# Attention and top-1 expert FFN on one core: the early experts' PSUM tiles, the first FFN rows' transposes, and the start of the weight stream

## The chip, the cores and the metric

The kernel runs on one core of a Trainium2 chip, in one launch. The metric is the device time of that core in microseconds (us), as the median of several runs. Each engine (TensorE = PE, VectorE = DVE, ScalarE = ACT, GpSimd = POOL, SyncE = SP) works through its own instructions in the order in which they were written, and waits at an instruction until the semaphores that it names have come.

## The reference

Long-range attention (a window of 32 keys to each side, plus 8 global positions) on 8 batches x 8 heads x 576 positions x 64, and then a feed-forward layer (FFN) in which each of the 4608 tokens goes to the one expert of eight with the highest logit:

```
x = attention(q, k, v)                      # 4608 rows of 512
logits = x @ w_gate;  e = argmax(logits);  g = softmax(logits)[e]
h = relu(x[rows of e] @ w1[e])              # 512 -> 1024
out[rows of e] = g * (h @ w2[e])            # 1024 -> 512
```

## The kernel before

**Attention and routing.** 36 steps of 128 query rows (lines 829 to 956) compute scores, exponentials and the weighted sum. Each step's output `xn` is transposed on PE (`xt_of`, line 487) and multiplied with the gate's weights (`gate`, `gates`), and a group of up to four steps is routed: DVE finds the maximum, `ranks` counts rows by expert with matmuls, `route2` turns counts into slots, `place` and `chunk` build one-hot matrices, `slots` adds them (on PE into a `tr_s` tile, then on DVE) into `acc`, a table from expert and slot to the row's place. `store` writes the rows to a scratch in DRAM, `xrow_scr`; `gather` (line 719) fetches the rows of a 128-row chunk with an indirect DMA from POOL, and `yscatter` (line 750) writes results to their tokens in the same way.

**Early experts.** The first 256 rows of experts 0 and 1 are known before the attention ends. Their FFN, `wave()` (line 779), is written as a generator, and `waves(n)` advances it by n pieces between the last groups' routing (lines 959 to 1002). A piece is one `hp` block (four matmuls of 256 columns and a relu on ACT, 16 in all) or half a `yw` block (four of eight matmuls of 512 columns, four blocks in all, each scaled by ACT into `y1`). The `hp` blocks rotate over three PSUM banks, of which two are halves of one tile; the four `yw` blocks take turns in the two banks of one tile:

```python
scw = scp.tile([128, 2, 512], FP32, tag="sc", name="hp")
hps = [scw[:, 0], gqp.tile([128, 512], FP32, tag="g", name="hp"), scw[:, 1]]
xw = xp.tile([128, 2, 512], FP32, tag="x", name="yw")
```

`wrows(i)` (line 969) transposes their gathered rows on PE into `tr_w` and copies them on ACT to `xts1`.

**From the wave to the FFN.** When the last groups are in `acc`, DVE computes `idx` (line 1001), the rows of every remaining chunk. After the wave, five weight pieces are fetched (`fetch`, line 1046: two DMAs of 256 KB from SP into an `st` tile), two chunks each of experts 0 and 1 are gathered, the wave's results are scattered, and expert 0's two chunks are transposed (`xtrans`, line 733, into `tx`) and copied by DVE to `xts`, which the first `h` matmul reads.

**The main FFN** (line 1209) goes over the eight experts: eight `h` blocks (fb 0 to 7, relu on ACT for even and on DVE for odd ones), between them the transposes for the next expert, then a `yp` block for each chunk (two chunks for experts 0 and 1, four for the others). From expert 2 on, `castp` (line 1053) casts a loaded piece to fp16 after odd fb and after each `yp` block, on ACT or DVE in turn, and fetches the next: 40 pieces for experts 3 to 7. `overflow_plan()` (line 1107), a generator too, works out on DVE which 128-row blocks are left beyond 512 rows of an expert; the loop advances it by one step after each fb in expert 2 and by two in experts 3 and 4. Its late steps transpose `acc` (line 1191), build three small `sel` matrices and multiply them on PE into `yi` (line 1199). The blocks left over run after the loop, in a chain of conditional parts (line 1305).

## Time and profile before

| | us |
|---|---|
| runs: lowest, median, highest of three | 393.03, 395.82, 397.62 |
| the profiled execution | 391.89 |
| its span, first to last instruction | 390.2 |
| PE busy, share of the span | 349.4 (90%) |
| DVE busy | 236.9 (61%) |
| POOL busy | 225.0 (58%) |
| ACT busy | 183.9 (47%) |

In the profile's rows a time is counted from the span's start. The row of a group of matmuls ends with the drain of its last one, in which the next row already begins. The idle time of an engine stands in brackets with what ended it; a wait for several semaphores is put down to the one that came last by the profile, which need not be the one that it stood for.

### The profile page before, as it was taken

Reading aid. Unit: us, or ns where it says so; the run is one execution under the profiler, and the core shown is the slowest. Engines: PE = TensorE matmul, PEld = TensorE weight load, DVE = VectorE, ACT = ScalarE, POOL = GpSimd, SP = SyncE. Lnnn points to the kernel's source line nnn. Section 1 sums busy time; section 2 is a strip of 40 time slices with the busy share of each in tenths; the row PEclk is TensorE's granted clock in tenths of the full one; section 3 lists DMA queues with packets and bytes.
Section 4 is the critical chain, followed back from the end, with each engine's and each line's share of the span. In section 5 each row is a group of like instructions: output and inputs, shape, how many; then the busy total and the mean of one; then the engine's idle time right before and its main releaser. Section 6 shows DMA issues by size and latency. Waiting matters only on the chain.

```text
span 390.2 us, 13139 instructions
## 1 busy us (share of the span) xinstructions
PE 349.4 (90%) x5290; PEld 224.7 (58%) x5290; DVE 236.9 (61%) x632; ACT 183.9 (47%) x310; POOL 225.0 (58%) x315
## 2 busy tenths in 40 slices
PE   6988989799898998989978878999899999999990
PEld 2557667566676776766656635654354444455550
DVE  8876876464957558777557504675875654333340
ACT  6636365553645455564535622264454445233330
POOL 8632676590746445394949466766466663565451
PEclk9999999999989999999999999999999999999997
DMA  7996969972899427999998885369999999132011
GB/s 192 225 256 114 270 114 235 229 181 62 181 271 212 130 67 164 260 204 203 169 166 169 166 252 188 109 203 360 356 342 355 368 372 329 37 117 83 22 38 49
DMA packets 90276, 76.29 MB, mean 196 GB/s; under 512 B 44380, under 2 KB 84956, under 8 KB 90208
## 3 DMA queue, kind: packets, MB, share of 16 engines
q1 hardware_dynamic: 79168, 54.34, 54.8%
q0 software_dynamic: 11040, 21.02, 21.6%
q8 instruction: 44, 0.72, 0.8%
q14 instruction: 24, 0.20, 0.2%
HBM read 68.62 MB, written 15.64 MB: 216 GB/s over the span
## 4 chain that ended last, share of the span: by engine, by line
PE 65%; DVE 10%; DMA 7%; issue 7%; POOL 6%; SPq 1%; ACT 1%; POOLq 0%; DVEq 0%
PE x L459 13%; PE yp L1242 12%; PE h L1224 11%; PE gx L546 5%; PE sc L459 4%; PE tr_x L491 4%; DMA wall<-in_k_dram 2%; PE poh L1275 2%; PE tr_k L524 2%; PE tr_l L506 2%; DMA wall<-in_q_dram 2%; PE tr_qk L340 2%; PE tr_qk L342 2%; POOL out_dram L751 2%; DVE xn L483 1%
## 5 line engine op out<-in xcount | busy, mean ns | idle before, releaser
L329 POOL CAST wall<-wall 128x768 f16<-128x768 f32 (+1 forms) x52 | 46.1, 903 | 40.5 <-DMA wall<-in_k_dram 23.6
L462 ACT ACTIVATE wall<-sc 128x1024 f32<-128x1024 f32 x36 | 36.9, 1025 | 54.4 <-PE sc L459 49.4
L682 POOL TENSOR_SCALAR hota<-ioc,chk,rowv 128x32 f16<-128x32 f16 (+8 forms) x33 | 34.4, 1070 | 36.1 <-DVE sm L654 36.0
L1224 PE MATMUL h<-xts,wall 128*128 128x512 f16 (+1 forms) x256 | 53.8, 352 | 0.8 <-DVE xts L741 0.8
L1242 PE MATMUL yp<-wall,ht 128*128 128x512 f16 x224 | 49.8, 379 | 1.7 <-DVE ht L764 1.7
L459 PEld LDWEIGHTS x<-wall 128*64 128x64 f32 x1152 | 37.6, 139 | 17.4 <-issue 15.5
L459 PE MATMUL x<-wall 128*64 128x65 f32 x1152 | 42.9, 227 | 3.1 <-issue 2.4
L751 POOL DMA_INDIRECT out_dram<-y,xr x24 | 25.1, 1048 | 24.5 <-DVE y L748 17.3
L1242 PEld LDWEIGHTS <-ht 128*128 128x128 f16 x224 | 21.5, 98 | 26.9 <-DVE ht L764 2.5
L1224 PEld LDWEIGHTS <-wall 128*128 128x128 f16 x256 | 23.9, 98 | 20.2 <-DVE xts L741 1.0
L481 DVE RECIPROCAL rz<-x 128x8 f32<-128x8 f32 x36 | 7.4, 207 | 42.3 <-PE x L459 42.1
L764 DVE TENSOR_SCALAR ht<-h 128x512 f16<-128x512 f32 (+1 forms) x32 | 19.9, 623 | 20.0 <-PE h L1224 18.1
L721 POOL DMA_INDIRECT xr<-xrow_scr,idx x24 | 25.9, 1080 | 9.0 <-POOL xr L720 9.0
L483 DVE TENSOR_TENSOR xn<-x,rz 128x512 f32<-128x512 f32 x36 | 24.9, 692 | 3.1
L766 ACT ACTIVATE ht<-h 128x512 f16<-128x512 f32 (+1 forms) x32 | 17.4, 542 | 19.1 <-PE h L1224 17.0
L492 ACT ACTIVATE xt<-tr_x 128x512 f32<-128x512 f32 (+1 forms) x37 | 22.0, 594 | 8.6 <-PE tr_x L491 8.5
L491 PE MATMUL tr_x<-id,xn 128*128 128x128 f32 x144 | 22.7, 280 | 3.7 <-DVE xn L483 3.6
L715 ACT ACTIVATE wall<-st 128x1024 f16<-128x1024 f32 x20 | 21.0, 1051 | 10.4 <-DMA st<-in_moe_w_dram 10.4
L459 PE MATMUL x<-vgd,ek 64*64 64x260 f32 x288 | 24.7, 404 | 0.0
L344 DVE COPY qt<-tr_qk 128x576 f16<-128x576 f16 x32 | 23.8, 750 | 0.7
L574 ACT ACTIVATE x16b<-xn 128x512 f16<-128x512 f32 x36 | 22.9, 636 | 0.0
L347 ACT ACTIVATE kt<-tr_qk 128x576 f16<-128x576 f16 x32 | 20.5, 646 | 4.6 <-PE tr_qk L342 4.6
(296 smaller groups left out, 702.1 us busy)
## 6 DMA issues: line engine op xcount, KB each, us to landing
st<-in_moe_w_dram SPq DMA_DIRECT2D x80, 256.0 KB
wall<-in_k_dram SPq DMA_DIRECT2D x32, 288.0 KB
wall<-in_q_dram SPq DMA_DIRECT2D x32, 288.0 KB
wall<-in_v_dram SPq DMA_DIRECT2D x24, 256.0 KB
wall<-in_moe_w_dram POOLq DMA_DIRECT2D x24, 256.0 KB, 6.9
xrow_scr<-x16b SPq DMA_DIRECT2D x8, 516.0 KB
wall<-in_v_dram SPq DMA_DIRECT2D x16, 192.0 KB
xg<-xgs SPq DMA_DIRECT2D x64, 2.0 KB
```

The lines of the kernel that those rows point to most:

```text
L329: eng.tensor_copy(o, i_)
L344: nc.vector.tensor_copy(qt[b % 2][:, pair, :].rearrange("p (a r) -> p a r", r=R), ps[:, 0:768].rearrange("p (r a) -> p a r", r=R)[:, 32:12 ...
L459: nc.tensor.matmul(out=o, lhsT=lhsT, rhs=rhs, start=first[r, g] == i, stop=final[r, g] == i)
L462: nc.scalar.activation(out=eb[s % 2].rearrange("p r t c q -> p r (t c q)"), in_=sc, func=AF.Exp, scale=0.125)
L483: nc.vector.tensor_tensor(out=xn.rearrange("p (c r d) -> p r c d", c=4, r=2), in0=x4[:, :, :, 0:D], in1=rz.rearrange("p r (c o) -> p r c o ...
L491: nc.tensor.transpose(out=ps[:, 128 * c : 128 * c + n], in_=xn[:, 128 * c : 128 * c + 128], identity=id32[0:n, 0:n])
L574: nc.scalar.activation(out=self.x16[:, s - self.s0, 0:DM], in_=xn, func=AF.Copy)
L682: eng.tensor_scalar(out=h[:, 0 : E * n].rearrange("p (e n) -> p e n", e=E), in0=ioc[:, :, 0:n], scalar1=self.chk[:, j : j + 1], scalar2=ro ...
L721: d_ = nc.gpsimd.indirect_dma_start(out=xr.bitcast(I16), out_offset=None, in_=xrow, in_offset=IndirectOffsetOnAxis(ap=ix, axis=0), bounds_ ...
L751: d_ = nc.gpsimd.indirect_dma_start(out=out, out_offset=IndirectOffsetOnAxis(ap=xr[:, DM : DM + 2].bitcast(I32), axis=0), in_=y, in_offset ...
L1224: nc.tensor.matmul(out=ps, lhsT=w1v[:, e, c, 128 * fb : 128 * fb + 128], rhs=xts[:, c, 0:N], start=(c == 0), stop=(c == 3))
L1242: nc.tensor.matmul(out=ps, lhsT=ht[:, fc, 128 * j : 128 * j + 128], rhs=w2v[:, e, fc, :], start=(fc == 0), stop=(fc == 7))
```

## The change

It makes six edits.

1. Four one-bank PSUM tiles (pool `ps_w`) take the place of the three tiles of the wave: every `hp` and `yw` block takes the next of the four. The pools are opened in another order for this.
2. The transpose of the last step's `xn` (`xt_of`) stands ahead of the first two `wrows`; one wave piece follows instead of two, then `gate` and the routing of the last group ahead of `wrows(2)` and `wrows(3)`. The pieces are counted out 1, 3, 6, 1 instead of 2, 3, 5, 2.
3. The gathers for experts 0 and 1 are written before the rest of the wave, and expert 0's two chunks are transposed at the end of the wave, the first ahead of the last `yw` block and the second behind it, through `tr_w` tiles into a fixed place in the weights' buffer (`xts0`).
4. The first five weight pieces are fetched one by one in experts 0 and 1 (after fb 3 and 7, and after expert 0's first `yp` block). Each waits for a one-column memset of its `st` tile on DVE.
5. The plan's steps: one after each of fb 0 to 6 in expert 2; from expert 3 on two after even fb, one after odd, none after fb 7.
6. In the FFN the pool of `tx` tiles is opened first.

```diff
-        scw = scp.tile([128, 2, 512], FP32, tag="sc", name="hp")
-        hps = [scw[:, 0], gqp.tile([128, 512], FP32, tag="g", name="hp"), scw[:, 1]]
         for e in range(NW):
             for fb in range(8):
-                ps = hps[(8 * e + fb) % 3][:, 0:HALF]
+                ps = wvp.tile([128, 512], FP32, tag="w", name="hp")[:, 0:HALF]
...
-        xw = xp.tile([128, 2, 512], FP32, tag="x", name="yw")
         for e in range(NW):
             for j in range(2):
-                ps = xw[:, j, :]
+                ps = wvp.tile([128, 512], FP32, tag="w", name="yw")
...
+    apx.close()
+    wvp = aps.enter_context(tc.tile_pool(name="ps_w", bufs=4, space=PS))
...
+    xt_of(xn, xt4[:, (NS - 1) % GB])
     wrows(0)
     wrows(1)
-    xt_of(xn, xt4[:, (NS - 1) % GB])
-    waves(2)
-    wrows(2)
-    wrows(3)
+    waves(1)
     gate(xt4[:, (NS - 1) % GB], tail.lg[:, 1, :])
     tail.route1()
     tail.block(NS - 1, xn)
+    wrows(2)
+    wrows(3)
     waves(3)
...
-    waves(5)
+    waves(6)
     done.slots()
-    waves(2)
+    waves(1)
     tail.slots()
...
-    waves(99)
+    for i in range(2 * NW):
+        gather(xr01[2 * NW + i], idx[:, i // 2, 2 + i % 2 : 3 + i % 2])
+    waves(11)
+    for j in range(2):
+        ps = trp.tile([128, 4, 128], FP16, tag="tr", name="tr_w")
+        xtrans(xr01[2 * NW + j], xts0[:, :, 128 * j : 128 * j + 128], ps)
+        waves(2)
+    for i in range(2 * NW):
+        yscatter(y1[i], xr01[i])
...
+            if len(loaded) < NST and len(pieces) >= 8 * (E - 3) - NST:
+                nc.vector.memset(st[:, 0:1], 0.0)
             wload(*p_, st)
...
-    for _ in range(NST):
-        fetch()
-    rows_of = {0: gathers(0), 1: gathers(1)}
-    for i in range(2 * NW):
-        yscatter(y1[i], xr01[i])
-    xts = fp2.tile([128, 4, 512], FP16, tag="xts", name="xts")
-    for j in range(NJ[0]):
-        xtrans(rows_of[0][j], xts[:, :, 128 * j : 128 * j + 128])
+    rows_of = {0: xr01[4:6], 1: xr01[6:8]}
+    xts = xts0
...
-            for _ in range(min(e - 1, 2) if e >= 2 else 0):
+            for _ in range(0 if e < 2 or fb == 7 else 1 if e == 2 or fb % 2 else 2):
                 next(plan, None)
             if fb % 2:
+                if e < 2 and fb % 4 == 3:
+                    fetch()
...
             yout(ps, rows_of[e][j], "act" if j % 2 else "dve")
+            if e == 0 and j == 0:
+                fetch()
```

At the start of the wave, ACT (`tr_w` are the gathered rows of the early experts, `tr_x` the last step's `xn`, `hp` the wave's relus, `x16b` a copy for the store) before:

```order
L739 ACTIVATE wall<-tr_w 128x4x128 x2
L492 ACTIVATE xt_84<-tr_x 128x512
L766 ACTIVATE wall<-hp 128x256 x2
L739 ACTIVATE wall<-tr_w 128x4x128 x2
L574 ACTIVATE x16b_81<-xn 128x512
L766 ACTIVATE wall<-hp 128x256 x3
L616 ACTIVATE ex<-d 128x16
L617 ACTIVATE x16b_81<-tokt 128x2
L766 ACTIVATE wall<-hp 128x256 x11
```

and after the change:

```order
L494 ACTIVATE xt_84<-tr_x 128x512
L741 ACTIVATE wall<-tr_w 128x4x128 x2
L768 ACTIVATE wall<-hp 128x256
L576 ACTIVATE x16b_81<-xn 128x512
L741 ACTIVATE wall<-tr_w 128x4x128 x2
L768 ACTIVATE wall<-hp 128x256 x3
L618 ACTIVATE ex<-d 128x16
L619 ACTIVATE x16b_81<-tokt 128x2
L768 ACTIVATE wall<-hp 128x256 x12
```

The copy of `tr_x` moves ahead of the first two `tr_w` copies, and only one relu instead of two stands ahead of the next two.

At the end of the wave, DVE (`idx` are the rows to gather, `xr` the row buffers of the main FFN, `ht` the relus of expert 0, `xts` the transposed rows of expert 1, `st` a weight piece) before, where the first two `xts` copies are those of expert 0:

```order
L731 SCALAR_TENSOR_TENSOR idx<-acc,idf 128x32
L1004 TENSOR_TENSOR cnt<-base_115,ebasef 128x8
L741 COPY xts<-tx 128x4x128 x2
L1037 MEMSET xr 128x258 x4
L764 TENSOR_SCALAR ht<-h 128x256
L741 COPY xts<-tx 128x4x128
L764 TENSOR_SCALAR ht<-h 128x256
L741 COPY xts<-tx 128x4x128
L764 TENSOR_SCALAR ht<-h 128x256 x2
L748 TENSOR_SCALAR y<-yp,wall 128x512
```

and after:

```order
L733 SCALAR_TENSOR_TENSOR idx<-acc,idf 128x32
L743 COPY wall<-tr_w 128x4x128 x2
L1013 TENSOR_TENSOR cnt<-base_115,ebasef 128x8
L1043 MEMSET xr 128x258 x4
L766 TENSOR_SCALAR ht<-h 128x256
L743 COPY xts<-tx 128x4x128
L766 TENSOR_SCALAR ht<-h 128x256
L1057 MEMSET st 128x1
L743 COPY xts<-tx 128x4x128
L766 TENSOR_SCALAR ht<-h 128x256 x2
L1057 MEMSET st 128x1
L750 TENSOR_SCALAR y<-yp,wall 128x512
```

Expert 0's two copies now come from `tr_w`; the row of 2 holds both, though PE has a `yw` block between their transposes. The small memsets that release the weight pieces stand behind relus of expert 0.

In the main FFN, DVE at the end of the plan (`acct` is the transposed `acc`, `ht` a relu, `wall<-st` a weight cast, `ov<-yi` reads the product), in expert 4 before:

```order
L1192 COPY acct<-tx 96x384
L1195 TENSOR_SCALAR sel<-ovs,colp 96x39
L764 TENSOR_SCALAR ht<-h 128x512
L1195 TENSOR_SCALAR sel<-ovs,colp 96x39 x2
L741 COPY xts<-tx 128x4x128
L1200 CAST ov_5330<-yi 128x39
L730 TENSOR_SCALAR lt<-ov_5330 128x39
L731 SCALAR_TENSOR_TENSOR ovi<-ov_5330,lt 128x39
L1203 CAST ovei<-ove 128x39
```

and in expert 5 after:

```order
L1194 COPY acct<-tx 96x384
L1197 TENSOR_SCALAR sel<-ovs,colp 96x39
L766 TENSOR_SCALAR ht<-h 128x512
L1197 TENSOR_SCALAR sel<-ovs,colp 96x39
L719 CAST wall<-st 128x1024
L743 COPY xts<-tx 128x4x128
L1197 TENSOR_SCALAR sel<-ovs,colp 96x39
L1202 CAST ov_5335<-yi 128x39
L732 TENSOR_SCALAR lt<-ov_5335 128x39
L733 SCALAR_TENSOR_TENSOR ovi<-ov_5335,lt 128x39
```

The third `sel` step now has a relu, a weight cast and an `xts` copy between it and the first, and nothing stands between it and the read of `yi`, whose matmuls follow directly behind an `h` block on PE.

## Rows read from the trace of the kernel before

**Rows 1.** The chain that ended last, in order of time (start us, us, what).
```profile
231.63 5.61 DMA out_dram<-wall
237.27 0.77 DVE xts L741 x2
```

**Rows 2.** Timeline of PE (start us, us, engine line op tiles xcount [idle before <-releaser]).
```profile
214.13 1.03 PE L786 MATMUL hp<-wall 128*128 128x256 f16 x8 [0.24 <-ACT wall L739]
...
229.59 1.89 PE L795 MATMUL yw<-wall 128*128 128x512 f16 x8 [0.82 <-ACT wall L746]
...
236.69 0.61 PE L737 MATMUL tx<-idh,wall 128*128 128x128 f16 x8
238.08 1.05 PE L1224 MATMUL h<-xts,wall 128*128 128x256 f16 x8 [0.78 <-DVE xts L741]
238.96 0.39 PE L737 MATMUL tx<-idh,wall 128*128 128x128 f16 x4
...
253.52 1.89 PE L1224 MATMUL h<-xts,wall 128*128 128x512 f16 x8
```

**Rows 3.** Waits of PE, 205 to 245 us (who <- whom: us in total, times, longest).
```profile
PE yw L795 <- ACT wall L746: 2.4, 3, 0.8
PE hp L786 <- ACT wall L766: 2.1, 5, 0.5
```

**Rows 4.** Timeline of DVE and of ACT around the early FFN.
```profile
211.68 0.69 DVE L483 TENSOR_TENSOR xn<-x,rz 128x512 f32<-128x512 f32 x1
...
225.02 0.19 DVE L731 SCALAR_TENSOR_TENSOR idx<-acc,idf 128x32 int32<-128x32 int16 x1
...
213.98 0.59 ACT L492 ACTIVATE xt<-tr_x 128x512 f32<-128x512 f32 x1
214.76 0.82 ACT L766 ACTIVATE wall<-hp 128x256 f16<-128x256 f32 x2 [0.20 <-PE hp L786]
...
236.94 0.69 ACT L746 ACTIVATE wall<-yw,wall 128x512 f32<-128x512 f32 x1 [2.03 <-PE yw L795]
```

**Rows 5.** Timeline of POOL: a gather, the last early scatter, a gather for expert 2.
```profile
225.98 1.14 POOL L721 DMA_INDIRECT wall<-xrow_scr,idx  x1 [6.96 <-DVE cnt L1004]
...
237.90 0.98 POOL L751 DMA_INDIRECT out_dram<-wall  x1 [1.73 <-ACT wall L746]
...
239.65 1.08 POOL L721 DMA_INDIRECT xr<-xrow_scr,idx  x1 [0.27 <-POOL xr L720]
```

**Rows 6.** Row gathers issued at 224 to 239 us, then 238 to 262.
```profile
DMA to landing us min/median/max: 5.3/6.2/6.3
...
DMA to landing us min/median/max: 2.7/2.9/3.6
```

**Rows 7.** Stretch 238 to 242 us: each engine's busy us, clock, DMA share, GB/s.
```profile
238.00:242.00 4.00, 3.89 (x38) 3.38 (x39) 3.05 (x10) 1.17 (x4) 3.45 (x9) 1.00 0.31 101
```

**Rows 8.** Expert 3: timeline of DVE, then of PE.
```profile
278.68 0.68 DVE L764 TENSOR_SCALAR ht<-h 128x512 f16<-128x512 f32 x1
...
279.42 5.57 PE L1242 MATMUL yp<-wall,ht 128*128 128x512 f16 x25 [1.72 <-DVE ht L764]
```

**Rows 9.** DVE: a step of the plan in expert 4, then expert 5.
```profile
290.69 0.23 DVE L1195 TENSOR_SCALAR sel<-ovs,colp 96x39 f16<-96x39 f32 x1
...
303.77 0.69 DVE L764 TENSOR_SCALAR ht<-h 128x512 f16<-128x512 f32 x1 [0.86 <-PE h L1224]
304.37 0.69 DVE L717 CAST wall<-st 128x1024 f16<-128x1024 f32 x1
```

**Rows 10.** Weight casts of experts 5 and 6 on ACT and DVE, then PE.
```profile
308.97 1.06 ACT L715 ACTIVATE wall<-st 128x1024 f16<-128x1024 f32 x1 [1.57 <-DMA st<-in_moe_w_dram]
...
325.76 1.06 ACT L715 ACTIVATE wall<-st 128x1024 f16<-128x1024 f32 x1 [2.31 <-DMA st<-in_moe_w_dram]
...
323.81 0.69 DVE L717 CAST wall<-st 128x1024 f16<-128x1024 f32 x1 [0.75 <-DMA st<-in_moe_w_dram]
...
329.30 1.89 PE L1224 MATMUL h<-xts,wall 128*128 128x512 f16 x8
```

More of the change, by code (lines that the diff above doesn't have):

```diff
@@ L110 @@
     aps = ExitStack()
-    scp = aps.enter_context(tc.tile_pool(name="ps_sc", bufs=1, space=PS))
-    xp = aps.enter_context(tc.tile_pool(name="ps_x", bufs=1, space=PS))
+    trp = aps.enter_context(tc.tile_pool(name="ps_tr", bufs=3, space=PS))
     gqp = aps.enter_context(tc.tile_pool(name="ps_g", bufs=1, space=PS))
-    trp = aps.enter_context(tc.tile_pool(name="ps_tr", bufs=3, space=PS))
+    apx = ExitStack()
+    scp = apx.enter_context(tc.tile_pool(name="ps_sc", bufs=1, space=PS))
+    xp = apx.enter_context(tc.tile_pool(name="ps_x", bufs=1, space=PS))
     qt = [ap_.tile([128, 4, S], FP16, name=f"qt{i}") for i in range(2)]
@@ L134 @@
     y1 = [wflat[:, kf_at + 1024 * i : kf_at + 1024 * (i + 1)].bitcast(FP32) for i in range(2 * NW)]
+    xts0 = wflat[:, 3 * 8192 : 3 * 8192 + 1024].rearrange("p (c n) -> p c n", c=4)
     xr01 = [wflat[:, 8 * 8192 - ROW * (i + 1) : 8 * 8192 - ROW * i] for i in range(8)]
@@ L981 @@
     tail.block(NS - 1, xn)
+    wrows(2)
+    wrows(3)
     waves(3)
     early.slots()
+    tail.ranks()
     tail.exps()
-    tail.ranks()
     tail.route2()
@@ L1015 @@
     fst = ctx.enter_context(tc.tile_pool(name="fst", bufs=NST))
+    pst = ctx.enter_context(tc.tile_pool(name="ps_t", bufs=2, space=PS))
     psh = ctx.enter_context(tc.tile_pool(name="ps_h", bufs=3, space=PS))
     psy = ctx.enter_context(tc.tile_pool(name="ps_y", bufs=3, space=PS))
-    pst = ctx.enter_context(tc.tile_pool(name="ps_t", bufs=2, space=PS))
     def new_rows():
@@ L1029, in gathers @@
         for j in range(NJ[e]):
-            if e < NW:
-                xr = xr01[2 * NW + 2 * e + j]
-            else:
-                xr = new_rows()
-                if fresh[0]:
-                    fresh[0] -= 1
-                    nc.vector.memset(xr, 0.0)
+            xr = new_rows()
+            if fresh[0]:
+                fresh[0] -= 1
+                nc.vector.memset(xr, 0.0)
             gather(xr, idx[:, e, NJ[5] - NJ[e] + j : NJ[5] - NJ[e] + j + 1])
```

## The prediction

> **What bounds the kernel now.** I read the page first: PE is busy for 90% of the span, so a gain has to come from the few places where it stands still or works late. The chain that ended last runs through PE nearly everywhere; in the passage from the early experts to the main FFN it leaves PE for a DMA of 5.61 us that "ends" at DVE's `xts` copy [rows 1]. That is one of several semaphores on which the copy waits. PE's timeline gives the nearer reason: the `tx` transposes begin at 236.69, at once behind the last `yw` block, and the copy starts 0.58 us later, about what a copy takes to follow its transposes [rows 1, 2]. So the passage is bound by PE's own order, and the question is why the wave ends so late.
>
> The waits answer that: three `yw` blocks wait 2.4 us in total for ACT's scaling of the block before, and five `hp` blocks 2.1 us for a relu [rows 3]. Each stands for a tile, not for data: the `yw` block at 229.59 writes the other bank of the tile that ACT is still reading [rows 2]. A wait costs more than its row, because the idle time is counted from the drain of the last matmul. The drain is 0.17: the `h` row at 238.08 lasts 1.05, yet the next row begins 0.88 later [rows 2]. A block of four 256-column matmuls is thus worth 0.44 and one of eight 512-column ones 1.72 (1.89 less 0.17, as at 229.59).
>
> **Part by part. One-bank tiles.** Three `yw` waits, 2.4 + 3 x 0.17 = 2.9; five `hp` waits, 2.1 + 5 x 0.17 = 2.95; together 5.9. What comes next in their place is ACT: two relus take 0.82, so 0.41 each against 0.44 for a block, and a scaling 0.69 against 1.72 [rows 4]. With four banks a block needs the evacuation of four blocks ago, so I leave nothing of the 5.9, except 0.2 in which the last group's ranks wait for DVE's one-hot rows, which now lie closer. Bounds: all 5.9 goes, or the `hp` half stays (2.95).
>
> **The last step's transpose sooner.** It needs `xn`, which DVE ends at 211.68 + 0.69 = 212.37; PE would start it at 212.5 and ACT copy it from 213.2 on, against 213.98 before [rows 4]. But the first two `tr_w` copies now stand behind it on ACT: three copies of about 0.55 (0.59 less overlap) end at 214.85, so the first `hp` starts at 214.9 instead of 214.13 [rows 2]: +0.8, with only one block instead of two ahead of the last group's `gate`. Bounds -0.2 to +1.0.
>
> **Transposes inside the wave.** Before, 1.39 us lie between the last `yw` block and the first `h` (236.69 to 238.08). Now one group of four transposes (0.22) stands ahead of the last `yw` block. Behind it come 0.22 for the other and then the later of two things: DVE's copy, and ACT's scaling of the last `yw` block, whose bank the first `h` takes over. The scaling ended 0.94 behind the block (236.94 + 0.69 - 236.69) [rows 2, 4], so `h` follows at about 1.0; 0.22 + 1.0 against 1.39 is -0.2.
>
> The two transposes must find their rows. `idx` is ready at 225.21 and the first gather starts 0.77 later [rows 4, 5]. The last group's table comes after ten `hp` blocks that no longer wait, by my count 1.6 earlier, so the first gather starts at 224.4 and the second, 1.5 later, at 225.9. Without weights in flight a gather landed 2.7 to 3.6 us after its issue, with them 5.3 to 6.3 [rows 6]. The second is wanted at about 231.8: three us of room at 2.9, and 0.4 too late at the worst 6.3. I take 0.
>
> Wave and passage together: -5.9 + 0.2 + 0.8 - 0.2 = -5.1, and the first `h` moves from 238.08 to 233.0.
>
> **Weight pieces later.** Five memsets of one column cost DVE nothing beside its idle time there. The fifth piece is released in the second expert, at about 233.0 + 7.7 + 3.7 = 244.4 (an early expert takes (253.52 - 238.08) / 2 = 7.7 [rows 2]). Expert 2 begins at 248.4 and casts that piece after eight `h` blocks of 0.86 and its first `yp` block, over 8 us later. The DMA share of 0.31 between 238 and 242 [rows 7] says that there is room for five pieces, so I take 0. What hides it is the slack of the stream: its pieces land 2.1 us apart ((325.76 - 308.97) / 8), and the last `w1` piece of expert 7 is cast at 324.5, 4.8 us before PE wants it at 329.30 [rows 10].
>
> POOL gains less than PE: its four scatters follow the four gathers, so the last moves from 237.90 to about 234.0, and the first gather for expert 2 from 239.65 to 235.8 [rows 5]. Expert 1 wants that row at 233.0 + 7.7 + 0.9 = 241.6, and the fourth, issued 1.4 apart and used 1.1 apart, with 4.9 us of room. At a landing of 2.9 nothing is late; at 6.3 the last is late by 1.4. What the trace shows with weights in flight is five pieces at once, which is not the case here, so I take 0 and keep 1.4 as the bound. The Trainium skill (DMA: Bandwidth & Descriptors, section "Issuing engines are not separate DMA queues") says that transfers of SP and of POOL run on the same DMA engines and interleave. By that rule the pieces that no longer slow the first gathers may slow these; the two rows on landings agree with it, and the sum would be 1.4 smaller.
>
> **The plan's steps.** In expert 3 PE waits 1.72 (1.9 with the drain) at the `yp` block because DVE reaches the last relu only at 278.68 [rows 8]. Of the fourteen steps ahead of that relu the last four (1.4 us) now come later, but the heavy six before them remain, and DVE meets the relu of fb 3 with less behind it and waits for the block. I count 0.5 gained; bounds 0 to 1.4.
>
> In expert 5 there is a new wait. Two steps at fb 4 bring the third `sel` and, directly after it, the `yi` matmuls on PE. On DVE that `sel` stands behind relu, second `sel`, cast and `xts` copy of fb 3. From the relu's start (303.77): 0.60 to the next, 0.15, 0.60 for the cast, 0.34 for the copy and 0.23 for the step [rows 9] give 305.69. PE leaves fb 3 at 303.6 and reaches `yi` after 0.22 + 0.86, at 304.7. The `h` blocks queued behind it wait too: +1.05. Bounds: 0 if PE is late by as much already, 1.5 if the cast waits for its piece. The `yi` and `acc` matmuls themselves only move from expert 4 to 5.
>
> **Sum.** -5.1 - 0.5 + 1.05 = -4.55. The profiled execution took 391.89 (span 390.2 and 1.7 around it), which makes 387.3. The median of the three runs lies 3.93 above that execution; from it the forecast is 395.82 - 4.55 = 391.3.
>
> **Rivals.** (a) *Expert 2's gathers come late.* For it: POOL moves by 3.9 and PE by 5.1. Against: 4.9 us of room and a landing of 2.9. Price 1.4: 392.7.
>
> (b) *The plan is spread as smoothly as it looks.* No stall at `yi`, and the whole 1.9 of expert 3 goes: -5.1 - 1.9 = -7.0, 388.8. For it: DVE waits for PE at the relu before (0.86 idle [rows 9]). Against: the order on DVE, where relu and cast stand ahead of the third `sel`.
>
> (c) *The passage hangs on the rows, as the chain says.* Then only the 1.6 of `idx` counts: -1.6 - 0.5 + 1.05, 394.8. For it: the 5.61 of rows 1. Against: PE began `tx` without waiting for any row [rows 2].
>
> (d) *Slower: the weight stream starts too late.* If the five pieces don't land before expert 2, the stream, which sets its own pace of 2.1, is behind by up to 5 x 2.1 = 10.5 in experts 5 and 6, and casts that wait on ACT and DVE hold up the relus behind them; three `h` banks cover two blocks, 1.7. That adds up to 8.8 and gives 395.82 - 4.55 + 8.8 = 400.1. It decides from about three missing pieces on, where 6.3 exceeds the slack of 4.8. For it: casts of experts 5 and 6 waited 0.75 to 2.31 already [rows 10]. Against: the count above, 4 us between the last release and expert 2. The Trainium skill (Trainium Kernel Development and Optimization, section "Best Practices") asks to overlap DMA with compute, which a later start gives up; by it this rival would be likelier, but the share of 0.31 says that the DMAs have idle time where the pieces go now.
>
> **Chances and range.** Forecast 0.55, own range 390 to 392.5; (a) 0.14; (b) 0.14; (c) 0.10; (d) 0.07. A measurement tells about 1%, here 3.96 us, from no change; three quarters of the forecast's cases pass it (it gains 4.55), and (b) does: 0.41 + 0.14 = 0.55 faster. The rest, (a) and (c) make 0.38 within 1%; (d) is the 0.07 slower. The range of 387.5 to 395.5 holds (a), (b), (c) and the spread of the runs, and leaves out (d).
>
> **What would show it.** Right: no PE wait on ACT in `yw` and `hp`; first `h` near 233; expert 3's stall near 1.2; a new PE wait of about 1 at `yi` in expert 5. Wrong: PE waits at `tx` in expert 1 (a), at `tr_w` ahead of the last `yw` (c), or in experts 5 to 7 behind casts that wait for pieces (d).

## The result and the profile after

Seven runs of the changed kernel gave a median of 389.88 us (388.25 to 396.82), seven of the kernel before 396.04 (391.56 to 398.42): ratio 0.9869, interval 0.983 to 0.9909, so 6.2 us by the medians and 5.2 by the ratio. The ratios, here and below, leave out every run that took over 1.5% more than the fastest of its kernel. The forecast was 391.3, in a range of 387.5 to 395.5. The profiled execution after, however, took 390.4 (span 388.7), only 1.5 less than the profiled one before. Both differences have to be explained.

First the waits of PE in the changed kernel, which answer to [rows 3] (who waits for whom: us in total, times, longest), from 205 to 245 us and then from 245 to 345.

```profile
PE hp L786 <- DMA wall<-in_moe_w_dram: 1.2, 1, 1.2
PE h L1226 <- ACT wall L748: 0.6, 1, 0.6
...
PE yp L1246 <- DVE ht L766: 1.0, 1, 1.0
PE yi L1201 <- DVE sel L1197: 1.0, 1, 1.0
PE tx L739 <- DVE st L1057: 0.5, 1, 0.5
```

The eight waits on ACT between blocks of the wave are gone. The first `h` waits 0.60 for ACT's scaling, as forecast; expert 3's stall is 1.00 instead of 1.72 [rows 8]; the new wait at `yi` is 0.97. Not forecast is the wait of 0.5 at `tx` in expert 1. Its row names a one-column memset on DVE, which happened to end at about the same time. What these transposes read are the rows of the fourth gather for expert 2, issued at 243.09 and landed 5.0 later, at 248.09; e5 below shows that it is the gather. But the first `h` comes at 235.75, not at 233.0. PE's timeline answers to [rows 2] (start us, us, engine line op tiles xcount [idle before <-releaser]):

```profile
211.31 1.04 PE L501 MATMUL tr_l<-wg,xt 128*128 128x8 f32 x8
212.72 0.63 PE L493 MATMUL tr_x<-id,xn 128*128 128x128 f32 x4 [0.37 <-DVE lg L502]
213.18 0.61 PE L739 MATMUL tr_w<-idh,wall 128*128 128x128 f16 x8
215.01 0.92 PE L786 MATMUL hp<-wall 128*128 128x256 f16 x4 [1.22 <-DMA wall<-in_moe_w_dram]
215.72 1.72 PE L501 MATMUL tr_l<-wg,xt 128*128 128x8 f32 x8
...
235.75 1.03 PE L1226 MATMUL h<-wall 128*128 128x256 f16 x8 [0.60 <-ACT wall L748]
...
248.15 0.40 PE L739 MATMUL tx<-idh,xr 128*128 128x128 f16 x4 [0.49 <-DVE st L1057]
```

The `hp` block at 215.01 starts where the forecast put it (214.9). Its wait of 1.22 is put down to a weight DMA, but it stands for ACT's copies of `tr_w`, the last of which ended at 213.88 + 1.08 = 214.96:

```profile
213.88 1.08 ACT L741 ACTIVATE wall<-tr_w 128x512 f16<-128x512 f16 x2
```

Then PE is slow: a group of `tr_l` matmuls of one form took 1.04 at 211.31 and takes 1.72 at 215.72. The windows say why (length; busy us and instruction counts of PE, PEld, DVE, ACT and POOL; then the granted clock, the DMA share and GB/s):

```profile
211.00:215.00 4.00, 2.42 (x34) 2.16 (x30) 3.52 (x17) 1.66 (x4) 4.00 (x6) 1.00 1.10 170
215.00:222.00 7.00, 6.99 (x42) 5.76 (x42) 2.15 (x10) 3.33 (x9) 4.23 (x4) 0.51 0.96 183
222.00:230.00 8.00, 8.00 (x64) 6.06 (x62) 3.88 (x19) 4.99 (x13) 2.21 (x3) 1.00 0.16 50
```

Behind two pauses, 0.37 and 1.22, TensorE was granted 0.51 for seven microseconds: nearly all of it at its lower level, 1.2 GHz instead of 2.4. That costs 7 x 0.49 = 3.4 of work at full clock, and the profiled execution before had nothing like it there. Below, "lost clock" is this sum: the length of a stretch times one minus its granted clock.

Landings of the row gathers answer to [rows 6] (issues, count, median us to landing): the early rows' and some of expert 2's, 224 to 239 us, then expert 2's, 238 to 244.

```profile
wall<-xrow_scr,idx POOLq DMA_INDIRECT x4, 2.6
out_dram<-wall POOLq DMA_INDIRECT x4
xr<-xrow_scr,idx POOLq DMA_INDIRECT x1, 3.9
...
st<-in_moe_w_dram SPq DMA_DIRECT2D x6, 256.0 KB
xr<-xrow_scr,idx POOLq DMA_INDIRECT x4, 4.5
```

The first four land in 2.6 instead of 5.3 to 6.3; expert 2's, which took 2.7 to 2.9, now take 4.5, the last one 5.0. The weight pieces have moved from the one group to the other. Where expert 2's gathers land, the DMAs are now full; in the same two windows before, their share was 0.36 and 0.31:

```profile
242.00:246.00 4.00, 4.00 (x36) 2.98 (x35) 2.91 (x11) 1.34 (x3) 3.12 (x5) 1.00 0.96 290
246.00:250.00 4.00, 3.51 (x30) 2.24 (x28) 1.89 (x6) 0.77 (x2) 3.17 (x7) 1.00 1.00 334
```

### The profile page after: what moved, and what is told of

It is laid out like the page before. It is cut to its first block, busy times and chain, and to the rows that moved or that the text cites. A ratio compares the mean times of both kernels' runs of the same rounds, so it can differ in the third digit from the quotient of the medians.

```text
span 388.7 us, 13144 instructions
## 1 busy us (share of the span) xinstructions
PE 354.1 (91%) x5290; PEld 228.9 (59%) x5290; DVE 243.3 (63%) x637; ACT 184.0 (47%) x310; POOL 226.4 (58%) x315
## 4 chain that ended last, share of the span: by engine, by line
PE 47%; DVE 15%; issue 14%; POOL 13%; DMA 8%; POOLq 1%; ACT 1%; SPq 0%; DVEq 0%; ACTq 0%
PE x L461 12%; POOL out_dram L753 6%; POOL xr L723 5%; DMA out_dram<-y,xr 5%; PE gx L548 5%; PE h L1226 5%; PE yp L1246 4%; PE sc L461 3%; PE tr_x L493 3%; PE hp L786 2%; PE tr_qk L342 2%; PE tr_k L526 2%; DVE xn L485 2%; DVE qt L346 2%; DVE wall L195 2%
## 5 line engine op out<-in xcount | busy, mean ns | idle before, releaser
L331 POOL CAST wall<-wall 128x768 f16<-128x768 f32 (+1 forms) x52 | 47.3, 924 | 36.4 <-DMA wall<-in_k_dram 19.2
L684 POOL TENSOR_SCALAR hota<-ioc,chk,rowv 128x32 f16<-128x32 f16 (+8 forms) x33 | 33.6, 1044 | 39.1 <-DVE sm L656 39.1
L1226 PE MATMUL h<-xts,wall 128*128 128x512 f16 (+1 forms) x224 | 49.7, 364 | 0.0
L494 ACT ACTIVATE xt<-tr_x 128x512 f32<-128x512 f32 (+1 forms) x37 | 22.0, 596 | 10.8 <-PE tr_x L493 10.8
```

The costliest lines, as they stand in the source:

```text
L331: eng.tensor_copy(o, i_)
L684: eng.tensor_scalar(out=h[:, 0 : E * n].rearrange("p (e n) -> p e n", e=E), in0=ioc[:, :, 0:n], scalar1=self.chk[:, j : j + 1], scalar2=ro ...
L1226: nc.tensor.matmul(out=ps, lhsT=w1v[:, e, c, 128 * fb : 128 * fb + 128], rhs=xts[:, c, 0:N], start=(c == 0), stop=(c == 3))
```

## The experiments

Three sets of four kernels, each set on one chip, each kernel in turn with the kernel before; ratios are to the kernel before of the same set, whose medians were 394.1, 394.4 and 405.58. Apart from e12, the changed kernel itself was in none of the three sets, so e1 to e8 are compared with it by their ratios. The table gives lengths from each profiled timeline, one execution of each kernel, which depend less on the execution than the total: the passage from the last group's `tr_lt` transpose to the first `h`, the clock lost in it, then from the first `h` to expert 2 (experts 0 and 1), and experts 2 to 6 from first `h` to first `h`. The passage before begins here:

```profile
208.61 0.33 PE L514 MATMUL tr_lt<-id,lt 128*128 128x128 f32 x1 [0.41 <-DVE lt L509]
```

| kernel | passage | lost clock | 0 and 1 | 2 | 3 | 4 | 5 | 6 | ratio, interval |
|---|---|---|---|---|---|---|---|---|---|
| before | 29.47 | 0 | 15.44 | 14.70 | 16.61 | 15.06 | 14.71 | 14.70 | |
| changed | 26.94 | 3.5 | 16.09 | 14.71 | 15.88 | 14.71 | 16.09 | 14.70 | 0.9869 (0.983, 0.9909) |
| e1_banks | 24.01 | 0 | 15.44 | 14.70 | 16.61 | 15.17 | 14.70 | 14.71 | 0.9887 (0.9832, 0.9942) |
| e2_oldorder | 23.12 | 0 | 16.88 | 14.70 | 15.95 | 14.70 | 15.99 | 14.71 | 0.9869 (0.9823, 0.9915) |
| e3_fill | 23.79 | 0 | 17.12 | 14.70 | 16.01 | 14.70 | 15.99 | 14.71 | 0.9845 (0.9794, 0.9895) |
| e4_yi | 26.95 | 3.5 | 16.46 | 14.71 | 15.88 | 14.71 | 15.12 | 14.71 | 0.9873 (0.9817, 0.9928) |
| e5_gfirst | 23.56 | 0 | 15.43 | 19.02 | 15.88 | 14.70 | 15.99 | 14.71 | 0.9974 (0.9926, 1.0023) |
| e6_early | 23.80 | 0 | 16.70 | 14.70 | 15.90 | 14.71 | 15.99 | 14.70 | 0.9851 (0.9793, 0.9909) |
| e7_combo | 23.79 | 0 | 15.42 | 18.75 | 16.08 | 14.71 | 15.12 | 14.71 | 0.9903 (0.9859, 0.9948) |
| e8_smooth | 23.82 | 0 | 15.42 | 18.82 | 14.71 | 14.70 | 15.07 | 15.53 | 0.9955 (0.9912, 0.9998) |
| e9_banks_smooth | 29.45 | 3.5 | 18.27 | 14.71 | 14.70 | 14.71 | 15.12 | 16.34 | 0.9964 (0.9925, 1.0002) |
| e10_late | 25.16 | 1.8 | 25.85 | 15.63 | 16.11 | 14.71 | 17.11 | 14.71 | 1.0027 (0.9981, 1.0074) |
| e11_split | 23.64 | 0 | 18.52 | 15.03 | 14.71 | 15.50 | 15.89 | 15.65 | 0.9898 (0.984, 0.9956) |
| e12_again | 26.51 | 3.5 | 25.36 | 15.33 | 16.09 | 14.70 | 16.06 | 14.71 | 1.0071 (1.003, 1.0113) |

**e1_banks: the one-bank tiles alone.** On the kernel before, with the order of the pools that goes with them (edit 6 too):

```
-        scw = scp.tile([128, 2, 512], FP32, tag="sc", name="hp")
-        hps = [scw[:, 0], gqp.tile([128, 512], FP32, tag="g", name="hp"), scw[:, 1]]
...
-                ps = hps[(8 * e + fb) % 3][:, 0:HALF]
+                ps = wvp.tile([128, 512], FP32, tag="w", name="hp")[:, 0:HALF]
...
-                ps = xw[:, j, :]
+                ps = wvp.tile([128, 512], FP32, tag="w", name="yw")
```

> The kernel before with one part of the change alone: the early experts' four one-bank tiles. Theory (false waits on two-bank tiles cost 5.9): no hp or yw block waits for ACT, the first h of the main FFN comes 5.7 earlier than in before (about 232.4), and the time is 5.7 below before, near 390.3, if the granted clock stays at 1.00 there. Rival (the passage hangs on the gathered rows): at most 1.6 gained, 394.4. Rival (the clock falls also here, since PE now runs through the same few microseconds): half of the gain is lost, about 393.

Measured: ratio 0.9887, 4.5 us of 394.1; the passage is 5.46 shorter. The first theory holds: this part alone makes nearly the whole gain (0.9887 against 0.9869), so the waits stood for tiles, not for data. (The edit also lets a block take the next of four banks instead of three for `hp` and two for `yw`; split tiles without more banks weren't run. For `yw` the row at 229.59 [rows 2] settles it, since that block writes a bank that nobody reads; for `hp` it is argued.) The profiled execution as a whole gained less than its passage (span 388.3 against 390.2): it had lost 5.1 us more to the clock before the passage (7 to 15 and 205 to 210 us), which began 3.7 later, at 212.28. The clock in the passage stayed at 1.00. The rows do now come late, but little (the next things to be waited for, in PE's timeline):

```profile
235.37 0.40 PE L738 MATMUL tx<-idh,wall 128*128 128x128 f16 x4 [0.62 <-DMA wall<-xrow_scr,idx]
236.29 1.05 PE L1224 MATMUL h<-xts,wall 128*128 128x256 f16 x8 [0.52 <-DVE xts L742]
```

**e2_oldorder: the order of before around the last step.** On the changed kernel:

```
-    xt_of(xn, xt4[:, (NS - 1) % GB])
     wrows(0)
     wrows(1)
-    waves(1)
+    xt_of(xn, xt4[:, (NS - 1) % GB])
+    waves(2)
+    wrows(2)
+    wrows(3)
...
-    wrows(2)
-    wrows(3)
...
-    waves(6)
+    waves(5)
```

> The changed kernel with the order of the kernel before around the last step: two groups of row transposes, then the xn transpose, then two hp blocks. Theory (the longer pause of PE ahead of the first hp is what the clock's fall to 0.50 follows): granted clock 1.00 between 215 and 222, hp blocks 0.44 again, about 3.0 back, and 0.8 less wait ahead of the first hp; against that a later gate. Time 2.5 to 3.5 below the changed kernel, near 387. Rival (the clock falls whatever the order, or the fall is a matter of the execution): time within 1 of the changed kernel, near 389.9; clock 0.5 again in that stretch.

Measured: 389.49 (387.98 to 390.58), ratio 0.9869, the changed kernel's own, so no difference that can be told; the clock in the passage is 1.00, and the passage is the shortest of all, 23.12. So the edit "x transpose sooner" costs some 0.4 to 0.7 of passage, as its sign was forecast. The 3.0 did not show in the time. In the profiled execution 0.8 of it goes to late gathers (expert 2 comes 16.88 after the first `h`, not 16.09), and the clock fell at another place, just ahead of the passage: 1.7 lost between 203 and 207.

**e3_fill: matmuls that nothing reads in the two pauses.** On the changed kernel:

```
+    def fill(n):
+        ps = wvp.tile([128, 512], FP32, tag="w", name="fill")
+        for _ in range(n):
+            nc.tensor.matmul(out=ps, lhsT=idh, rhs=w1v[:, 0, 0, 0:512], start=True, stop=True)
+    fill(1)
     xt_of(xn, xt4[:, (NS - 1) % GB])
     wrows(0)
     wrows(1)
+    fill(5)
     waves(1)
```

> The changed kernel with six matmuls more that nothing reads (512 columns each, one ahead of the xn transpose, five ahead of the first hp), so that PE works through the two pauses of 0.37 and 1.22. Theory (the pause is what the clock falls after): granted clock 1.00 between 215 and 222, the fillers are hidden in the pauses (6 x 0.21 = 1.3 against 1.6), time about 3.0 below the changed kernel, near 386.9. Rival (the fall has another cause): the clock near 0.5 again and the time within 1 of the changed kernel, or above it by what the fillers cost at the lower clock.

Measured: 388.09 (386.12 to 390.65), the lowest median of the set, 1.4 to 2.0 below its three neighbours; the intervals overlap. By the ratios it is 0.9 below the changed kernel, where 3.0 were expected. The first filler does not fill its pause, it waits 0.29 itself; the other five leave PE no idle time ahead of the first `hp`. The window of the stretch that had 0.51:

```profile
215.00:222.00 7.00, 7.00 (x73) 6.26 (x72) 4.96 (x23) 5.66 (x16) 3.65 (x4) 1.00 0.93 197
```

And PE's timeline in expert 1, which has two waits instead of one:

```profile
243.74 0.40 PE L739 MATMUL tx<-idh,xr 128*128 128x128 f16 x4 [0.66 <-DMA xr<-xrow_scr,idx]
245.44 0.40 PE L739 MATMUL tx<-idh,xr 128*128 128x128 f16 x4 [0.43 <-DMA xr<-xrow_scr,idx]
```

Experts 0 and 1 take 17.12 instead of 16.09. That is not mainly PE coming sooner: from the first gather to the first `h` it took 7.97 here, 8.15 in e2 and 8.24 in the changed kernel, so PE is at most 0.3 earlier against POOL. The rest is longer landings, up to 5.5 here and 5.7 in e2 against 5.0; and e4, whose passage is that of the changed kernel to 0.01, still took 16.46. The late gathers thus cost 0.65 to 1.7 from one execution to another.

Over all thirteen profiles that have the wave's new tiles, the clock fell within the first blocks of the wave in four of the six with the pause of 1.22 (changed, e4, e10, e12; not in e5 and e6), in none of the four with fillers (e3, e7, e8, e11), and in one of the three with the old order (e9). That speaks for the pause as a cause, but one of seven without it against four of six with it doesn't show it, and it isn't the only thing that decides. Nor do the set's times: the mean granted clock of six runs each was 0.987 in e3, 0.982 in e2, 0.979 in e1 and 0.978 in e4, so e1, which lacks the pause, is no better than e4, which has it.

**e4_yi: one plan step less at fb 4 of expert 5.** On the changed kernel:

```
-            for _ in range(0 if e < 2 or fb == 7 else 1 if e == 2 or fb % 2 else 2):
+            for _ in range(0 if e < 2 or fb == 7 else 1 if e == 2 or fb % 2 or (e == 5 and fb == 4) else 2):
```

> The changed kernel with one step of the overflow plan less at fb 4 of expert 5, so that the yi matmuls come one h block later than the third sel. Theory (the new stall of 0.97 at yi is PE waiting for that sel on DVE): the wait is gone, time about 1.0 below the changed kernel, near 388.9. Rival (the wait only moves, to the next relu or cast on DVE): a wait of the same size at a later h or yp block of expert 5, and time within 0.5 of the changed kernel.

The `yi` matmuls of this kernel, which the third `sel` no longer holds up:

```profile
299.00 1.89 PE L1226 MATMUL h<-xts,wall 128*128 128x512 f16 x8
300.72 0.41 PE L1201 MATMUL yi<-sel,acct 96*128 96x39 f16 x3
```

Expert 5 takes 15.12 instead of 16.09, and no new wait appears: the theory holds. The time, 390.04 (386.69 to 393.94), can't show a microsecond.

**e5_gfirst: expert 2's gathers ahead of the early scatters.** On the changed kernel:

```
-    for i in range(2 * NW):
-        yscatter(y1[i], xr01[i])
...
             rows_of[e + 2] = gathers(e + 2)
+            if e == 0:
+                for i in range(2 * NW):
+                    yscatter(y1[i], xr01[i])
```

> The changed kernel with the four scatters of the early experts issued behind the gathers for expert 2 instead of ahead of them, so that these gathers leave POOL some 5.3 sooner and ahead of the weight pieces. Theory (PE's waits at tx in expert 1, which make the stretch from the first h to the start of expert 2 16.1 to 17.1 long instead of the 15.44 of before, are gathers that come late): the stretch is 15.44 again, landings of these gathers near 3, time 0.7 to 1.7 below the changed kernel, near 388.7. Rival (the waits come from DVE or PE, or the scatters now hold up something): the stretch stays over 16, or a wait of like size shows elsewhere; time within 0.5 of the changed kernel.

Measured: 393.91 (389.24 to 399.24), ratio 0.9974, by the ratios 4.1 above the changed kernel, a time that neither theory nor rival gave. By stages both hold. Experts 0 and 1 take 15.43 again, so the waits there were late gathers (the memsets of `st` stayed where they were). But expert 3's gathers, now behind four scatters, come late in expert 2. PE's timeline, and the window of 6.00 us behind the pause with its granted clock of 0.72:

```profile
252.50 0.40 PE L739 MATMUL tx<-idh,xr 128*128 128x128 f16 x4 [2.46 <-DMA xr<-xrow_scr,idx]
```

```profile
252.00:258.00 6.00, 5.50 (x24) 2.60 (x25) 2.92 (x7) 1.18 (x3) 4.83 (x7) 0.72 0.57 189
```

Expert 2 takes 19.02: 2.46 of wait and 6 x 0.28 = 1.7 of clock are most of the 4.3 more. POOL's timeline gives the reason:

```profile
228.83 1.00 POOL L723 DMA_INDIRECT wall<-xrow_scr,idx  x1 [0.27 <-POOL wall L722]
233.77 1.05 POOL L723 DMA_INDIRECT xr<-xrow_scr,idx  x1 [0.68 <-POOL xr L722]
...
247.17 1.05 POOL L723 DMA_INDIRECT xr<-xrow_scr,idx  x1 [0.27 <-POOL xr L722]
```

A gather or a scatter takes up POOL for 1.3 to 1.6, and from 224 to 254 it works without a break but for the 3.9 between the first two of these rows, where the gathers wait for DVE's memsets of their rows. In the changed kernel scatters fill that time.

**e6_early: all five pieces at the start, as before.** On the changed kernel:

```
-            if len(loaded) < NST and len(pieces) >= 8 * (E - 3) - NST:
-                nc.vector.memset(st[:, 0:1], 0.0)
...
+    for _ in range(NST):
+        fetch()
     rows_of = {0: xr01[4:6], 1: xr01[6:8]}
...
-                if e < 2 and fb % 4 == 3:
-                    fetch()
...
-            if e == 0 and j == 0:
-                fetch()
```

> The changed kernel with the five first weight pieces fetched at once ahead of expert 0, as in the kernel before. Theory (a gather that shares the DMAs with pieces lands 5 to 6 after its issue instead of 2.6 to 3.3, and the edit only moved that from the gathers of the early rows to those of expert 2): landings near 6 for the first four gathers and near 2.8 for expert 2's; 15.44 from the first h to expert 2; against it a PE wait of 0 to 1 at the tr_w ahead of the last yw blocks; time 0.3 to 1.5 below the changed kernel, near 389. Rival (the order of the pieces doesn't matter to the gathers, POOL's own order does): 16.1 to 17.1 from the first h to expert 2 still, time as the changed kernel's or above it.

Landings in this kernel, of the early rows and then of expert 2's, and in a second fence PE's timeline:

```profile
wall<-xrow_scr,idx POOLq DMA_INDIRECT x4, 5.5
...
xr<-xrow_scr,idx POOLq DMA_INDIRECT x4, 3.3
```

```profile
237.09 0.40 PE L739 MATMUL tx<-idh,wall 128*128 128x128 f16 x4 [0.89 <-DMA wall<-xrow_scr,idx]
```

The landings turn round as the theory says: who shares the DMAs with the pieces lands late. But the wait turns round as well: the second early expert's rows are late in expert 0, and experts 0 and 1 take 16.70. The forecast of 15.44 was wrong, and the time can't decide: the ratio of 0.9851 rests on four of the twelve runs, while the median of all twelve, 392.2, lies 2.2 below the kernel before's 394.4, a ratio of 0.994. The edit "weight pieces later" thus moves a cost of about one microsecond from one group of gathers to the next. The rule of the Trainium skill that the prediction weighed (DMA: Bandwidth & Descriptors, section "Issuing engines are not separate DMA queues") agrees with these two rows and with those of the changed kernel.

**e7_combo and e8_smooth: mends together.** e7 has the edits of e3, e4 and e5; e8 also spreads the plan:

```
+    NPL = [[0] * 8, [0] * 8, [1] * 7 + [0], [2, 1, 2, 1, 1, 1, 0, 0], [2, 2, 2, 2, 2, 2, 1, 0], [2, 2, 2, 2, 1, 1, 1, 0]]
...
-            for _ in range(0 if e < 2 or fb == 7 else 1 if e == 2 or fb % 2 else 2):
+            for _ in range(NPL[e][fb] if e < 6 else 2):
```

> The changed kernel with three mends together: expert 2's gathers ahead of the early scatters, one plan step less at fb 4 of expert 5, and the six idle matmuls in the two pauses of PE. Theory: 1.0 (yi) and 1.3 (gathers) less, and the low clock behind the pauses seldom or never seen, worth up to 3.4 in an execution that had it: median 3 to 4 below the changed kernel, near 386. Rival (the mends hide behind each other, what comes next is late by as much): 388.5 or above.

> The same three mends, and the plan's steps spread again: none at fb 6 and 7 of expert 3 and one at fb 2 to 5 less there, more in expert 4. Theory (expert 3's stall of 1.00 is DVE being late at the last relu for the plan's steps before it): the stall falls from 1.00 to 0.3 or less, time 0.7 to 1.0 below the kernel with three mends alone, near 385. Rival (expert 4 pays for it, since its DVE gets the steps): expert 4 longer than 14.71 by as much, no difference to the kernel with three mends.

Measured: medians of 391.07 and 392.5. Both miss in time (e8 lies above e7, not below), since both carry e5's wait (2.19 and 2.48) and the low clock behind it, some 4 in expert 2. By stages, e8's theory holds: expert 3 falls from 16.08 to 14.71 and expert 4 stays at 14.70. But expert 6 grows by 0.8. ACT waits there for a weight piece, and a relu waits behind the cast:

```profile
317.47 1.06 ACT L717 ACTIVATE wall<-st 128x1024 f16<-128x1024 f32 x1 [1.86 <-DMA st<-in_moe_w_dram]
318.44 1.07 ACT L768 ACTIVATE ht<-h 128x512 f16<-128x512 f32 x2
...
319.07 1.02 PE L1235 MATMUL h<-xts,wall 128*128 128x512 f16 x4 [0.66 <-ACT ht L768]
```

**e9 to e12, on a chip with gaps.** e9 is e1 with e8's plan; e12 is the changed kernel unaltered; the other two, on the changed kernel (e11 has e3's edit and e8's plan too):

```
e10_late
-                if e < 2 and fb % 4 == 3:
-                    fetch()
+                if e == 1 and fb % 4 == 3:
+                    for _ in range(2 + fb // 7):
+                        fetch()
...
-            if e == 0 and j == 0:
-                fetch()

e11_split
-    for i in range(2 * NW):
+    for i in range(2):
         yscatter(y1[i], xr01[i])
...
             rows_of[e + 2] = gathers(e + 2)
+            if e == 1:
+                for i in range(2, 2 * NW):
+                    yscatter(y1[i], xr01[i])
```

> The kernel before with two things alone: the four one-bank tiles, and the plan's steps spread as in the kernel with all mends and smooth steps (expert 3 lighter at its end, expert 4 heavier, the yi matmuls at fb 5 of expert 5). The weight pieces, the transposes and the order ahead of the wave stay as before. Theory (the banks are worth 5.4, expert 3's stall 1.9, and the change's other parts give back in late gathers what they gain): 7.0 to 7.5 below before, ratio near 0.981, and 2 to 3 below the changed kernel. Rival (the weight stream, which the casts of experts 5 and 6 already wait for, holds the relus up as soon as expert 3 is faster): a new PE wait of 0.5 to 2 in expert 6, gain 5.5 or less.

> The changed kernel with its five first weight pieces all released in the second expert (two at fb 3, three at fb 7), so that none is in flight while the gathers for expert 2 land. Theory (pieces in flight are what makes these gathers land in 5 instead of 3): landings near 2.8, the stretch from the first h to expert 2 back at 15.44; in exchange the stream of pieces, which sets its own pace of 2.1, starts some 8 later and runs out of slack: PE waits in experts 5 to 7 behind casts, 2 to 6 in total, time 1 to 5 above the changed kernel. Rival (POOL's order alone makes the gathers late): 16.1 to 17.1 still.

> The changed kernel with the six idle matmuls, the smooth plan, and two of the early experts' four scatters moved behind the gathers for expert 3 (the other two stay ahead of the gathers for expert 2). Theory (POOL is full there: its first 3 idle microseconds take two scatters for nothing, four moved scatters made expert 3's gathers 2.5 late, two fewer cost nothing): 15.44 from the first h to expert 2, no tx wait over 0.5 in expert 2, expert 3 at 14.71, time 3 to 4 below the changed kernel, near 386. Rival (the weight stream is the next bound): the time won shows up again as PE waits behind casts in experts 5 and 6, gain 2 or less.

> The changed kernel as it is, timed once more beside the others. By the terms measured so far at full clock (passage 5.9 less, late gathers 1.4 to 1.7 more, plan 0.3 more) it should be 4.1 below before, ratio near 0.990; by the first comparison 0.987. If stretches at the lower clock fall at the same place in this execution again, ahead of or in the early experts, the pause of 1.22 ahead of the first hp is a likely cause; if elsewhere, they belong to the execution.

In this set the kernel before took 405.58, eleven more than on the other chips, and all four profiles show DVE, in e10 and e12 ACT too, and PE behind them, idle for nothing that the profile names ("issue" and "remote"). In e12, DVE, ACT and then PE:

```profile
246.95 0.42 DVE L766 TENSOR_SCALAR ht<-h 128x256 f16<-128x256 f32 x1 [2.46 <-issue]
249.09 0.42 DVE L743 COPY xts<-tx 128x512 f16<-128x512 f16 x1 [1.72 <-remote]
251.29 0.42 DVE L766 TENSOR_SCALAR ht<-h 128x256 f16<-128x256 f32 x1 [1.78 <-remote]
...
250.54 0.38 ACT L768 ACTIVATE ht<-h 128x256 f16<-128x256 f32 x1 [5.95 <-remote]
...
250.97 1.86 PE L1226 MATMUL h<-wall 128*128 128x256 f16 x8 [5.17 <-issue]
```

PE goes on at 250.97, 0.05 behind the end of ACT's relu. Between 200 and 262 us such gaps on DVE sum to 8.4, 7.9, 7.9 and 10.8 in e9 to e12, and to 0.3 at most in the ten profiles from other chips. (In e9 a further 7.86 is marked in the same way, but DVE's copy follows 0.58 behind PE's `tx`, as it does in the kernel before.) In e9, e11 and e12 some 4.5 of it lies in the last attention steps, ahead of the passage, and in e9 another 2.8 ahead of the first `h`, where PE stood for 3.54; the rest falls into experts 0 and 1. These take 18.3 to 25.9 instead of 15.4 to 17.1, each kernel by another amount, so this set's ratios say more of the gaps than of the edits. On this chip the changed kernel is slower than before, 1.0071. Its experts 0 and 1 take 25.36 here instead of 16.09, 5.17 of it in one gap; without such gaps the ratio was 0.9869. e10's question, what the gathers cost with no piece in flight, stays open, since its gap of 6.0 in expert 0 hides them. The waits behind casts that its text expected in experts 5 to 7 did not come (PE waits there only at `yi`, 2.00), but the gaps gave the late pieces time too. In e12 the clock fell in the passage again, by 3.5. The kernel before has no profile from that chip, so whether it has gaps of the same size there, and why the changed kernel loses more to them, stays open.

By stages two things can be read. e9 brings expert 3 to 14.70, 1.9 less than before, and hands 1.6 of it back in expert 6, as its rival said, again behind a cast (its row names no piece, but the casts on ACT before and after it, at 322.20 and 330.71, wait for theirs):

```profile
326.71 1.06 ACT L716 ACTIVATE wall<-st 128x1024 f16<-128x1024 f32 x1 [2.39 <-issue]
...
328.30 1.02 PE L1225 MATMUL h<-xts,wall 128*128 128x512 f16 x4 [1.47 <-ACT wall L716]
```

And e11 has no `tx` wait in expert 2 with two scatters moved instead of four; but its experts 0 and 1 took 18.52, which gave the gathers 3 us more, so this doesn't show that two scatters cost nothing. Of this set it is the fastest: its interval, 0.984 to 0.9956, lies below both before and the changed kernel beside it (1.003 to 1.0113), from six runs. It wasn't run on a chip without gaps.

## Why the prediction was right, and where it wasn't

The total was right to 1.4 us, in part by luck: two errors of about one cancelled, and on the third chip, where the changed kernel came out at 1.0071, no such gain was seen. Term by term, from the table, at full clock:

- **One-bank tiles.** Forecast -5.9, and 0.2 left. Alone they gave -5.46 of passage (e1), with the rows' wait of 0.62 taking some. Right: the `hp` half of the waits went as well as the `yw` half.
- **The last step's transpose sooner.** Forecast +0.8; the first `hp` came 6.20 behind `tr_lt` instead of 5.52 (+0.7), and undoing the order gave 0.4 (e5's passage, 23.56, without low clock, against e2's 23.12). Right in sign and nearly in size. What the step left out is the clock: behind this pause it fell in four profiles of six, in the profiled execution for 3.5 in the passage. That the pause makes it fall was not shown.
- **Transposes inside the wave.** From first `yw` to first `h` it took 8.12 instead of 11.21: -3.09, where -2.9 (the `yw` waits) and -0.2 were forecast. Right. In e1, whose transposes stand behind the wave and wait for their rows, it took 8.83.
- **Passage together.** Forecast -5.1; measured 23.56 to 23.80 (e5, e6) against 29.47, so -5.7 to -5.9 at full clock, and -2.5 with the low one. Most of the 0.6 to 0.8 more lies between the first `hp` and the first `yw`: 12.74 before, 9.36 in e5 and 9.47 in e6, thus -3.3 to -3.4 where -2.95 + 0.2 was counted.
- **Weight pieces later, and expert 2's gathers: 0.** This is the step that failed. It was argued that the DMA share of 0.31 leaves room and that the five pieces are not in flight at once; with them the share is 0.96 to 1.00, and they are in flight enough. The order on POOL was forecast nearly right: the fourth gather was issued at 243.09 and its rows were wanted at 247.5 (the wait and a drain of 0.17 ahead of 248.15), 4.4 of room instead of 4.9. What was wrong is the landing, taken at 2.9 and measured at 3.9 to 5.0. It cost 0.65 in the profiled execution, 1.0 in e4 and 1.4 to 1.7 in e2 and e3. Moving the gathers (e5) or the pieces (e6) away took the waits in expert 1 away. Rival (a), at 0.14 and 1.4, had the mechanism and the size. The other half of the step held: no cast waits long enough to hold up PE in experts 5 to 7.
- **The plan in expert 3.** Forecast -0.5, measured -0.73. Right.
- **The stall at `yi`.** Forecast +1.05, the wait measured 0.97, and e4 took it away. Right. Expert 5 grew by 1.38, since besides the wait the 0.35 of `yi` and `acc` moved there from expert 4, as the prediction said.

The sum at full clock, with the passage of e5, is -5.9 + 0.65 to 1.68 - 0.73 - 0.35 + 1.38, that is -3.9 to -5.0; forecast -4.55. Passage and gathers are the two errors that cancelled, which is luck. The profiled execution gained only 1.5 because 3.5 of clock lay in its passage; and before's profiled execution, 391.89, is near the fastest of its runs, so that pair shows the change too small, and the medians, 6.2 apart, a little too large.

Of the rivals, (b) was excluded by the wait at `yi`, (c) by e1's 5.46 where it allowed 1.6. Rival (d) didn't come about: the only PE wait in experts 5 to 7 is `yi`. But its mechanism is the next bound: each time expert 3 was made faster by the smoother plan, expert 6 grew (e8, e9, e11), in e8 and e9 behind a cast. In the kernel before the DMA share is 1.06 to 1.07 from 300 to 330 us already.

## What to carry to other kernels

Look at what a wait's tile shares, not only at what the instruction reads: two banks in one tile made eight waits that no data asked for, and splitting them alone was worth 5.5 us of the stage and 4.5 by the ratio. Moving a burst of transfers out of one stage's way means checking by its landing times which stage it lands in next; here the cost changed owner and stayed near one microsecond. And before a pause of PE is accepted as "0.8 for an earlier copy", look at what the granted clock does behind it, in more than one execution.

## What the runs showed of the hardware

The lower clock comes in portions. But for the last microseconds, where PE is done, a fall lost 1.7, 3.4 or 5.1 us in every profile (sums over slices of one us of one minus the granted clock), at different places in different executions of one kernel: the same passage of the changed kernel lost 3.5 in two profiles out of two, that of e5 and e6, with the same pause, nothing. Behind the waits of 2.2 to 2.5 in expert 2 it fell in three profiles of three (e5, e7, e8); behind that of 1.72 in expert 3 of the kernel before it did not. The Trainium skill (TensorE: Matmul & The Clock Gate, section "What's actually happening") says that the gate follows how busy the array has lately been, with two levels only; the windows of 0.51 and 1.00 agree. The spread between runs of one kernel goes with it: over the kernel before's 36 runs of the second set the mean granted clock ran from 0.958 to 0.995 and the time from 390.6 to 405.1, longer the lower the clock (correlation -0.82). A change worth one or two per cent is better read by stages than by one execution's total.

The gaps of the third chip were unexpected too: DVE took one instruction every 2.1 to 2.2 us (246.95, 249.09, 251.29) with nothing to wait for that the trace names, and ACT stood for 5.95 ahead of the relu behind which PE went on. What held the two up there stays open.
